# Softmax of the first two batches in five blocks, and signs, low parts and additions made by GpSimd

## The chip, the cores and the metric

The kernel runs on one core of a Trainium2 chip. The metric is the device time of one execution in microseconds (us). TensorE (PE) multiplies and has its weights loaded by a path of its own (PEld); VectorE (DVE), ScalarE (ACT) and GpSimd (POOL) do the elementwise work; SyncE (SP) issues nearly all transfers. Each engine runs its own instructions in program order and waits on semaphores for the others.

## The reference

All tensors are float32. For 8 batches of 8 heads, 576 positions and head size 64, keys and values are pooled into 32 slots per head; queries attend to the slots; the result goes through a feed-forward layer of width 2048.

```python
a = softmax(phi, axis=2)                          # phi (8, 8, 576, 32)
k_m = einsum('bhsm,bhsd->bhmd', a, k)             # v_m the same with v
attn = softmax(q @ k_m.T / sqrt(64))              # (8, 8, 576, 32)
x = (attn @ v_m).transpose(0, 2, 1, 3).reshape(4608, 512)
h = x @ w_in                                      # w_in (512, 2048)
g = where(h > 0, h, exp(min(h, 0)) - 1)
out = g @ w_out                                   # w_out (2048, 512)
```

`w_in` and `w_out` arrive as float64; the kernel reads them as pairs of 32-bit words.

## The kernel before, in words

**Products.** The value product and `w_in` are fused: for each batch `vw` multiplies the pooled values with `w_in`, and `hidden` multiplies the attention weights `A` with `vw`. `hidden` and `project` are made three times over split operands: a high part that ScalarE rounds, and a low part, the difference, that VectorE subtracts (`vw_high` and `vw_low`, `probs_high` and `probs_low`, `elu_high` and `elu_low`, `dec_high` and `dec_rest`). The passes run low weights first, then the low part of the moving side, then both high.

**Steps.** One iteration `it` is a batch, a half of its positions and a tile `j` of 128 hidden channels: `hidden.it` (6 matmuls of 288 columns, L672), `elu_exp.it` (ScalarE, L687 and L688), `elu_max.it` (VectorE, L696), `rest_copy.it` (GpSimd copies the last 32 positions away, L715), `elu_high.it` (ScalarE, L719), `elu_low.it` (VectorE, L725), `project.it` (6 matmuls of 512 columns, L733). 256 iterations follow each other.

**Weights.** Tile `k` (32 of them, `w_in` and `w_out`) comes by `load_raw.k` as float64 words. `dec_mag.k` (ScalarE, L376) scales the upper word; `dec_top.k` (VectorE) takes its sign bit (L384) and ors it to the shifted magnitude (L385); `dec_low.k` (ScalarE, L380) scales the lower word; `dec_add.k` (VectorE, L397) adds it as an integer; for `w_out`, `dec_high.k` (ScalarE, L404) rounds and `dec_rest.k` (VectorE, L409) subtracts. Tiles 0 to 7 are `w_in` 0, `w_out` 0, `w_in` 1 and so on to `w_out` 3.

**Attention of batches 0 and 1.** The pooled keys come from `slots` (L465), `slots_copy` (L482), `slots_transpose` (L499) and `kv_copy` (L506), first for the keys (`K`) and then for the values (`V`) in batch 0. `scores.b.u` (L514) multiplies queries of unit `u`; then on VectorE `turn` (32x32 transposes, L547), `softmax_max` (L554), `softmax_shift` (L562), on ScalarE `softmax_exp` (L566), on VectorE `softmax_sum` (L572, L573, L575), `softmax_divide` (L583), `turn_back` (L589), then `probs_high` (L606) and `probs_low` (L614). Units are ranges of positions: `units(b)` gives four of 160, 128, 160 and 128 for batches 0 and 1, three of 192 for the others. A unit's scores have two halves side by side, so a unit of 160 is worked on as 320 elements.

**Order.** The string `FIRST` writes out the order of all steps of the first 64 iterations by hand; the rest comes from rules. Steps of one engine run in the order in which they stand. `warm_up.n` is n matmuls of the identity on TensorE (L812), whose results nobody reads; each shows as two records. `ph`, `kvt`, `raw` and `qh` are transfers that SP issues in order.

**Tuples.** `shift_on_pool`, `low_on_pool` and the like name units whose step GpSimd does instead of VectorE; all of them are empty.

Of the kernel before, what the change touches and what calls it, by code (L numbers as in the profile page):

```python
# [47 lines left out]
tables load_phi.0 load_kv0.K0 load_kv0.K1 load_kv0.T phi_max.0.0 load_raw.0 phi_exp.0.0  # L48
phi_max.0.1 phi_exp.0.1 load_half_q.0.0 warm_up.11 e_transpose.0.0 slot_scale.0 e_transpose.0.1
e_copy.0.0 load_kv0.V0 slots.0.0.K.y e_copy.0.1 e_transpose.0.2 slots.0.1.K e_copy.0.2 load_kv0.V1  # L50
slots.0.2.K slots.0.3.K dec_mag.0 slots.0.4.K load_raw.1 slots_copy.0.K dec_top.0 warm_up.2
slots_transpose.0.K kv_copy.0.K dec_low.0 load_raw.2 warm_up.1 scores.0.0.yz scores.0.1 turn.0.0
turn.0.1 softmax_max.0.0 warm_up.2 slots.0.0.V.y load_phi.1 softmax_max.0.1 slots.0.1.V
softmax_shift.0.0 softmax_shift.0.1 softmax_exp.0.0 dec_add.0 softmax_exp.0.1 load_raw.3 warm_up.1
slots.0.2.V softmax_sum.0.0 slots.0.3.V softmax_sum.0.1 slots.0.4.V load_raw.5 softmax_divide.0.0
dec_mag.1 softmax_divide.0.1 turn_back.0.0 slots_copy.0.V turn_back.0.1 load_half_q.0.1
probs_high.0.0 warm_up.3 slots_transpose.0.V dec_top.1 probs_high.0.1 dec_mag.2 probs_low.0.0
kv_copy.0.V dec_low.1 load_kv.1.0 warm_up.3 vw.0.0.0.128.yz probs_low.0.1 dec_top.2
vw_high.0.0.0.128 load_kv.1.1 vw_low.0.0.0.128 dec_low.2 dec_add.1 warm_up.4 hidden.0 dec_mag.3
dec_add.2 dec_high.1 load_raw.6 dec_top.3 vw.0.0.128.256 elu_exp.0 dec_mag.5 dec_rest.1  # L60
load_kv.1.2 dec_low.3 elu_max.0 scores.0.2.yz phi_max.1 vw_high.0.0.128.256 rest_copy.0
scores.0.3.hh elu_high.0 load_kv.1.3 vw_low.0.0.128.256 phi_exp.1.0 turn.0.2 load_kv.1.4
phi_exp.1.1 turn.0.3 load_raw.4 softmax_max.0.2 hidden.1 softmax_max.0.3 softmax_shift.0.2
e_transpose.1.0 softmax_shift.0.3 elu_exp.1 load_raw.7 slot_scale.1 dec_add.3 softmax_exp.0.2
# [906 lines left out]
```

## Time and profile before

| | us |
|---|---|
| median of 3 runs (lowest, highest) | 722.78 (721.74, 724.0) |
| the profiled execution | 722.7 |
| its span, first to last instruction | 720.9 |
| TensorE busy | 700.8 (97%) |
| VectorE busy | 465.0 (64%) |
| ScalarE busy | 460.7 (64%) |
| GpSimd busy | 45.6 (6%) |

1.8 us of the profiled execution lie outside its span. Busy shares are means over stages with different limits: the first 65 us are unlike the rest.

### The profile page before, as it was taken

To read this page: it belongs to the slowest core of one execution; us is meant where nothing else is said; L and a number is where in the kernel's file an instruction comes from. 1 tells how busy PE (TensorE), PEld (TensorE's weight loads), DVE (VectorE), ACT (ScalarE), POOL (GpSimd) and SP (SyncE) were. 2 spreads that over 40 slices of the span, in tenths; PEclk is the share of its full clock that TensorE was granted. 3 is DMA by queue.
4 is the path that set the end of the run, shared out by engine and by line. 5 is a ranking of instruction groups with operands and counts; after the bars stand their busy time and mean duration, and the time that the engine had idled before them with its cause. 6 is when DMAs were issued, how large, how long until landed. Compare 5 with 4: busy or idle time off the path is not lost.

```text
span 720.9 us, 13704 instructions
## 1 busy us (share of the span) xinstructions
PE 700.8 (97%) x5114; PEld 575.8 (80%) x5114; DVE 465.0 (64%) x1253; ACT 460.7 (64%) x1110; POOL 45.6 (6%) x88
## 2 busy tenths in 40 slices
PE   7698999999999999999999999999999999999997
PEld 6576888888767888888887888888878888788886
DVE  3999899887495548664773547854593545945442
ACT  3778998886546756675564755765564655656652
POOL 0001112112100100010000100001000010000000
PEclk8799999999999999999999999999999999999999
DMA  8960503432312710343003430046000360000001
GB/s 304 367 257 9 226 30 117 151 104 63 103 60 81 184 51 1 96 135 101 0 1 110 132 104 1 0 109 193 30 1 33 85 197 31 1 30 1 30 1 45
DMA packets 24978, 64.46 MB, mean 89 GB/s; under 512 B 3408, under 2 KB 7632, under 8 KB 24912
## 3 DMA queue, kind: packets, MB, share of 16 engines
q1 hardware_dynamic: 24816, 63.46, 27.6%
q8 instruction: 41, 0.67, 0.4%
q14 instruction: 25, 0.20, 0.1%
q10 hardware_dynamic: 96, 0.13, 0.1%
...
## 4 chain that ended last, share of the span: by engine, by line
PE 87%; DVE 8%; DMA 2%; ACT 1%; issue 1%; SPq 0%; POOL 0%; DVEq 0%; POOLq 0%; ACTq 0%
PE pso L733 53%; PE psh L672 27%; PE psb L514 3%; PE psb L465 2%; PE pso L514 2%; DMA kvt<-kvt 1%; DMA e<-phi 1%; DVE gf L696 1%; DVE top L385 1%; DVE sm L572 1%; DVE vw L634 0%; DVE top L397 0%; DMA nmd<-nm 0%; DVE gp L725 0%; DVE mx L554 0%
## 5 line engine op out<-in xcount | busy, mean ns | idle before, releaser
L733 PE MATMUL pso<-wout,gp 128*128 128x512 f32 x1728 | 448.4, 397 | 3.7 <-DVE gp L725 2.3
L733 PEld LDWEIGHTS pso<-wout,gp 128*128 128x128 f32 x1728 | 309.0, 188 | 69.6 <-DVE gp L725 4.2
L672 PEld LDWEIGHTS psh<-A,vw 128*128 128x128 f32 x1536 | 230.9, 189 | 36.8 <-issue 10.2
L672 PE MATMUL psh<-A,vw 128*128 128x288 f32 x1536 | 248.7, 297 | 3.6 <-DVE spare L547 1.9
L699 DVE SCALAR_TENSOR_TENSOR gf<-gf,psh 128x256 f32<-128x256 f32 x192 | 80.7, 420 | 145.3 <-ACT gf L688 145.0
L687 ACT ACTIVATE gf<-psh 128x288 f32<-128x288 f32 x256 | 104.8, 409 | 106.6 <-PE psh L672 104.8
L719 ACT CAST gp<-gf 128x256 fp32r<-128x256 f32 x256 | 103.5, 405 | 81.2 <-DVE gf L699 65.9
L725 DVE TENSOR_TENSOR gp<-gf,gp 128x256 fp32r<-128x256 f32 x256 | 109.1, 427 | 50.2 <-ACT gp L719 49.5
L688 ACT ACTIVATE gf<-gf 128x288 f32<-128x288 f32 x256 | 113.9, 445 | 8.1
L290 POOL TENSOR_TENSOR e<-e,nmb 128x512 f32<-128x512 f32 (+1 forms) x18 | 20.8, 1180 | 367.9 <-DMA nmb<-nmd 204.0
L696 DVE SCALAR_TENSOR_TENSOR gf<-gf,psh 128x288 f32<-128x288 f32 x64 | 28.9, 452 | 17.4 <-ACT gf L688 16.2
L715 POOL COPY rest<-gf 128x32 f32<-128x32 f32 x64 | 24.3, 379 | 167.3 <-DVE gf L696 167.3
L707 DVE SCALAR_TENSOR_TENSOR rest<-gf,psh 128x32 f32<-128x32 f32 x192 | 34.6, 180 | 0.0
L634 DVE TENSOR_TENSOR vw<-psb,vw 128x512 fp32r<-128x512 f32 (+2 forms) x52 | 28.4, 569 | 1.9 <-ACT vw L628 1.8
L777 ACT CAST gp<-rest 128x256 fp32r<-128x256 f32 x32 | 12.6, 405 | 24.2 <-PE pso L733 22.5
L628 ACT CAST vw<-psb 128x512 fp32r<-128x512 f32 (+2 forms) x52 | 23.7, 486 | 0.7 <-PE psb L514 0.7
L514 PE MATMUL psb<-win,kvm 64*32 64x512 f32 (+2 forms) x416 | 23.8, 511 | 0.3 <-DVE win L397 0.3
L782 DVE TENSOR_TENSOR gp<-rest,gp 128x256 fp32r<-128x256 f32 x32 | 13.1, 419 | 16.2 <-ACT gp L777 16.1
L385 DVE SCALAR_TENSOR_TENSOR top<-mag,top 128x512 uint32<-128x512 uint32 x32 | 22.2, 692 | 1.9 <-ACT mag L376 0.3
L380 ACT ACTIVATE mag<-raw 128x512 uint32<-128x512 uint32 x30 | 20.0, 670 | 3.3 <-DVE top L385 3.3
L376 ACT ACTIVATE mag<-raw 128x512 f32<-128x512 f32 x30 | 19.5, 665 | 0.4 <-DVE win L397 0.4
L634 DVE TENSOR_TENSOR vw<-pso,vw 128x512 fp32r<-128x512 f32 (+1 forms) x26 | 16.0, 620 | 0.0
...
## 6 DMA issues: line engine op xcount, KB each, us to landing
...
```

The source lines that it names most:

```text
L385: nc.vector.scalar_tensor_tensor(t, mags[k].bitcast(U32), 3, t, ALU.logical_shift_left, ALU.bitwise_or)
L514: nc.tensor.matmul(outs[a][32 * j : 32 * j + 32, :], lhs[r, 32 * j : 32 * j + 32], rhs[r, j], start=True, stop=True, tile_position=(64 * a ...
L634: nc.vector.tensor_tensor(t[:, LO, a, n0:n1], s["ps"]["vw", c, n0][a], t[:, HI, a, n0:n1], ALU.subtract)
L672: nc.tensor.matmul(ps, t[:, x, g, c0 : c0 + P], s["A"][hf][:, y, g, :], start=(n == 0), stop=(n == 5),)
L687: nc.scalar.activation(gf, ps, AF.Relu, scale=-1.0)
L688: nc.scalar.activation(gf, gf, AF.Exp, scale=-1.0)
L696: nc.vector.scalar_tensor_tensor(gf, gf, -1.0, ps, ALU.add, ALU.max)
L699: nc.vector.scalar_tensor_tensor(gf[:, :n], gf[:, :n], -1.0, ps[:, :n], ALU.add, ALU.max)
L707: nc.vector.scalar_tensor_tensor(rest_of(b, j)[:, o : o + REST], gf[:, n:], -1.0, ps[:, n:], ALU.add, ALU.max)
L719: nc.scalar.copy(gp[:, HI], gs[it][:, : NT * P])
L725: eng.tensor_tensor(gp[:, LO], gf[:, : NT * P], gp[:, HI], ALU.subtract)
L733: nc.tensor.matmul(ps, gp[:, y], wout[j][:, x, :], start=(first and n == 0), stop=(last and n == 2),)
```

## The change

- `units` gives batch 0 three units (160, 128 and 288 positions) and batch 1 two of 288: five blocks in place of eight.
- The sign of a weight tile is a step of its own, `dec_sign.k`. For 19 tiles GpSimd makes it as the upper word, read as float32, times zero, which leaves a zero with the word's sign. The other 13 keep the mask on VectorE. It is written to where the tile will stand, so that `dec_top` and `dec_add` work in place.
- `dec_rest` is done by GpSimd for 8 of 16 tiles of `w_out`, `dec_add` for 6 of 32 tiles. Three of five `probs_low` and one `softmax_shift` of batches 0 and 1 go to GpSimd too.
- `FIRST` is written anew.

```diff
+    shift_on_pool = ((1, 0),)
+    low_on_pool = ((0, 0), (0, 2), (1, 0))
+    rest_on_pool = (1, 3, 7, 14, 15, 23, 29, 30)
+    sign_on_pool = (1, 3, 7, 9, 10, 11, 15, 16, 17, 19, 20, 21, 22, 23, 24, 26, 27, 29, 30)
+    add_on_pool = (0, 20, 23, 24, 26, 30)
...
     def units(b):
-        if b < NB:
-            return (0, 160), (160, 288), (288, 448), (448, 576)
+        if b == 0:
+            return (0, 160), (160, 288), (288, 576)
+        if b == 1:
+            return (0, 288), (288, 576)
         return (0, 192), (192, 384), (384, 576)
...
+    def dec_sign(k):
+        t = made(k)
+        word = raws[k][:, :, 1].rearrange("p (r n) -> p r n", r=NPAIR)
+        if k in sign_on_pool:
+            nc.gpsimd.tensor_scalar(t, word.bitcast(F32), 0.0, None, ALU.mult)
+        else:
+            nc.vector.tensor_scalar(t.bitcast(U32), word, 0x80000000, None, ALU.bitwise_and)
+
     def dec_top(k):
-        t = t2k([P, CW], "top").bitcast(U32)
-        nc.vector.tensor_scalar(t, raws[k][:, :, 1], 0x80000000, None, ALU.bitwise_and)
+        t = made(k).bitcast(U32)
+        mag = mags[k].bitcast(U32).rearrange("p (r n) -> p r n", r=NPAIR)
         nc.vector.scalar_tensor_tensor(
-            t, mags[k].bitcast(U32), 3, t, ALU.logical_shift_left, ALU.bitwise_or
+            t, mag, 3, t, ALU.logical_shift_left, ALU.bitwise_or
         )
...
+        eng = nc.gpsimd if k in add_on_pool else nc.vector
+        eng.tensor_tensor(t, t, lows.pop(k).rearrange("p (r n) -> p r n", r=NPAIR), ALU.add)
...
+        eng = nc.gpsimd if k in rest_on_pool else nc.vector
+        t = tops.pop(k).rearrange("p r n -> p (r n)")
+        eng.tensor_tensor(w[:, LO, :], t, w[:, HI, :], ALU.subtract)
```

Three places show what `FIRST` and the tuples move. Lines of the changed kernel stand some 15 higher than before.

TensorE, from the last key slots of batch 0 (`kvt,spare`) over the transpose of the pooled keys (`ident,spare`) to its first scores (`qh,kvm`), before:

```order
L465 MATMUL pso_133<-kvt,spare 32x64 x32
L812 MATMUL pso_84<-ident 128x128 x2
L499 MATMUL psb<-ident,spare 128x128
L812 MATMUL pso_84<-ident 128x128
L514 MATMUL pso_199<-qh,kvm 32x160 x4
```

and in the changed kernel:

```order
L480 MATMUL pso_134<-kvt,spare 32x64 x24
L827 MATMUL pso_84<-ident 128x128 x5
L514 MATMUL psb<-ident,spare 128x128
L529 MATMUL pso_204<-qh,kvm 32x160 x4
```

Five identity matmuls stand ahead of the transpose where two stood, and none behind it. SP's queue changes there too: the transfer of the last slots' rows (`kvt`) went ahead of the first weight tile (`win_78`) before:

```order
L311 DMA kvt<-kv 128x1024 x2
L309 DMA kvt<-kvt 64x1024
L368 DMA win_78<-w_in 128x1024
L340 DMA qh<-q 128x1152
```

and goes behind it in the changed kernel:

```order
L311 DMA kvt<-kv 128x1024 x2
L368 DMA win_78<-w_in 128x1024
L309 DMA kvt<-kvt 64x1024
L340 DMA qh<-q 128x1152
```

VectorE, from the sums of batch 0's last softmax to `elu_low.0` (`gp<-gf,gp`), before (two units of 160 and 128 positions):

```order
L572 TENSOR_REDUCE sm<-spare 128x8
L573 TENSOR_SCALAR sm<-sm 128x8
L575 RECIPROCAL rs<-sm 128x8
L583 TENSOR_TENSOR spare<-spare,rs 128x320
L409 TENSOR_TENSOR wout_485<-top,wout_485 128x512
L583 TENSOR_TENSOR spare<-spare,rs 128x256
L589 STREAM_TRANSPOSE spare<-spare 128x320
L589 STREAM_TRANSPOSE spare<-spare 128x256
L384 TENSOR_SCALAR top<-raw 128x512
L385 SCALAR_TENSOR_TENSOR top<-mag,top 128x512
L614 TENSOR_TENSOR A<-spare,A 128x2x160
L384 TENSOR_SCALAR top<-raw 128x512
```

and in the changed kernel (one unit of 288):

```order
L598 TENSOR_TENSOR spare<-spare,rs 128x576
L604 STREAM_TRANSPOSE spare<-spare 128x576
L397 TENSOR_SCALAR top<-raw 128x512
L402 SCALAR_TENSOR_TENSOR top<-mag,top 128x512
L397 TENSOR_SCALAR win_77<-raw 128x4x128
L402 SCALAR_TENSOR_TENSOR win_77<-mag,win_77 128x4x128
L740 TENSOR_TENSOR gp<-gf,gp 128x256
```

`dec_rest.3` (`wout_485`) and `probs_low` are gone from between them. They stand on GpSimd, whose queue began with `rest_copy` before and now begins like this (`A<-spare,A` is `probs_low`, `wout` is `dec_rest`, TENSOR_SCALAR is `dec_sign`, `win_80<-win_80,mx` is `softmax_shift.1.0`):

```order
L409 TENSOR_TENSOR win_77<-win_77,mag 128x4x128
L395 TENSOR_SCALAR top<-win_78 128x512
L629 TENSOR_TENSOR A<-spare,A 128x2x160
L395 TENSOR_SCALAR top<-raw 128x512
L423 TENSOR_TENSOR wout_362<-top,wout_362 128x512
L629 TENSOR_TENSOR A<-spare,A 128x576
L423 TENSOR_TENSOR wout_457<-top,wout_457 128x512
L730 COPY rest<-gf 128x32 x2
L395 TENSOR_SCALAR top<-raw 128x512
L730 COPY rest<-gf 128x32 x2
L577 TENSOR_TENSOR win_80<-win_80,mx 128x576
L395 TENSOR_SCALAR win_78<-raw 128x4x128
```

Some copies moved far back: `rest_copy.18` now stands behind `elu_high.41`, `rest_copy.32` behind `elu_max.45`.

## Rows read from the trace of the kernel before

**Rows 1.** Busy time of each engine in three stretches (us from the span's start), with its number of instructions, then the granted TensorE clock, the DMA share and GB/s.

```profile
15.00:65.00 50.00, 40.02 (x509) 30.39 (x494) 48.57 (x138) 36.12 (x90) 2.75 (x9) 0.86 0.69 250
70.00:180.00 110.00, 109.97 (x698) 90.08 (x698) 94.80 (x201) 92.61 (x217) 20.05 (x46) 1.00 0.36 114
230.00:710.00 480.00, 480.00 (x3335) 402.19 (x3334) 279.70 (x812) 293.35 (x714) 17.42 (x15) 1.00 0.21 62
```

**Rows 2.** Timeline of PE from 39 to 65 us: start, duration, what, count, and in brackets the idle time before it and what ended it. The row at 39.55 is `hidden.3`, those at 46.92 and 49.49 are `hidden.5` and `hidden.6`, those at 59.36 and 63.78 are `project.5` and `project.6` from their second matmul on.

```profile
39.55 1.15 PE L672 MATMUL psh<-A,vw 128*128 128x288 f32 x6
...
46.92 1.06 PE L672 MATMUL psh<-A,vw 128*128 128x288 f32 x6 [0.37 <-DVE gf L696]
...
49.49 1.13 PE L672 MATMUL psh<-A,vw 128*128 128x288 f32 x6 [0.86 <-DVE vw L634]
...
59.36 1.43 PE L733 MATMUL pso<-wout,gp 128*128 128x512 f32 x5 [1.27 <-DVE gp L725]
...
63.78 1.43 PE L733 MATMUL pso<-wout,gp 128*128 128x512 f32 x5 [1.06 <-DVE gp L725]
```

**Rows 3.** Timeline of VectorE at three points: the first `turn`, `elu_low.0` and `elu_low.6`.

```profile
15.00 0.35 DVE L547 STREAM_TRANSPOSE spare<-pso 128x160 f32<-128x160 f32 x1 [1.39 <-PE pso L514]
...
39.76 0.42 DVE L725 TENSOR_TENSOR gp<-gf,gp 128x256 fp32r<-128x256 f32 x1
...
63.31 0.41 DVE L725 TENSOR_TENSOR gp<-gf,gp 128x256 fp32r<-128x256 f32 x1
```

**Rows 4.** Timeline of PE from 11 to 24 us: the last key slots, identity matmuls, the transpose of the pooled keys, the first scores, and identity matmuls behind the first `vw` product.

```profile
11.27 0.43 PE L465 MATMUL pso<-kvt,spare 64*32 64x64 f32 x16 [0.59 <-DMA kvt<-kvt]
11.63 1.15 PE L812 MATMUL pso<-ident 128*128 128x128 f32 x4
13.34 0.47 PE L499 MATMUL psb<-ident,spare 128*128 128x128 f32 x1 [0.56 <-ACT spare L482]
...
14.17 0.79 PE L514 MATMUL pso<-qh,kvm 64*32 64x160 f32 x16
...
22.66 1.16 PE L812 MATMUL pso<-ident 128*128 128x128 f32 x8
```

**Rows 5.** Timeline of ScalarE: the first `dec_mag`, which waited for the first weight tile.

```profile
12.21 0.67 ACT L376 ACTIVATE mag<-win 128x512 f32<-128x512 f32 x1 [3.13 <-DMA win<-w_in]
```

**Rows 6.** Busy time by stretch as in rows 1, for two stretches of half clock.

```profile
11.70:18.50 6.80, 6.24 (x89) 4.63 (x93) 4.59 (x13) 3.29 (x8) 0.00 (x0) 0.50 1.02 408
28.90:39.00 10.10, 7.56 (x84) 6.44 (x87) 9.46 (x31) 8.10 (x19) 0.21 (x1) 0.50 1.03 334
```

**Rows 7.** Groups of VectorE instructions by line and shape, from 15 to 65 us: count, busy time, mean ns of one, idle time before.

```profile
L397 DVE CUSTOM_DVE_ANT_0 win<-top,mag 128x1024 uint16<-128x1024 uint16 x4 | 2.7, 684 | 0.0
L409 DVE TENSOR_TENSOR wout<-top,wout 128x512 fp32r<-128x512 f32 x4 | 2.7, 682 | 0.0
L384 DVE TENSOR_SCALAR top<-raw 128x512 uint32<-128x512 uint32 x6 | 2.5, 415 | 0.0
L614 DVE TENSOR_TENSOR A<-spare,A 128x320 fp32r<-128x320 f32 x2 | 1.0, 484 | 0.0
L614 DVE TENSOR_TENSOR A<-spare,A 128x256 fp32r<-128x256 f32 x2 | 0.8, 420 | 0.0
L573 DVE TENSOR_SCALAR sm<-sm 128x8 f32<-128x8 f32 x4 | 0.7, 172 | 0.1
L575 DVE RECIPROCAL rs<-sm 128x8 f32<-128x8 f32 x4 | 0.8, 204 | 0.1
```

**Rows 8.** Groups of VectorE by line and shape over the whole span: `softmax_max` of 384 and of 256 elements.

```profile
L554 DVE TENSOR_REDUCE mx<-sc 128x12 f32<-128x384 f32 x18 | 9.8, 545 | 0.0
L554 DVE TENSOR_REDUCE mx<-spare 128x8 f32<-128x256 f32 x2 | 0.8, 408 | 0.0
```

**Rows 9.** Groups of GpSimd by line and shape over the whole span.

```profile
L715 POOL COPY rest<-gf 128x32 f32<-128x32 f32 x64 | 24.3, 379 | 167.3 <-DVE gf L696 167.3
L290 POOL TENSOR_TENSOR e<-e,nmb 128x512 f32<-128x512 f32 x12 | 16.1, 1365 | 367.9 <-DMA nmb<-nmd 204.0 <-ACT gf L687 86.9 <-DVE gp L725 74.6
L290 POOL TENSOR_TENSOR e<-e,nmb 64x256 f32<-64x256 f32 x6 | 4.9, 811 | 0.0
```

**Rows 10.** Timelines of GpSimd and of VectorE around 320 us: three additions of GpSimd (two of 512 elements, one of 256, the last two in one row), and the `elu_low` of VectorE before and beside them.

```profile
319.13 1.31 POOL L290 TENSOR_TENSOR e<-e,nmb 128x512 f32<-128x512 f32 x1 [74.39 <-DMA nmb<-nmd]
320.39 2.21 POOL L290 TENSOR_TENSOR e<-e,nmb 128x512 f32<-128x512 f32 x2
...
318.83 0.43 DVE L725 TENSOR_TENSOR gp<-gf,gp 128x256 fp32r<-128x256 f32 x1
...
320.75 1.24 DVE L725 TENSOR_TENSOR gp<-gf,gp 128x256 fp32r<-128x256 f32 x1 [0.38 <-ACT gp L719]
```

**Rows 11.** Timelines of GpSimd and VectorE at 83 and at 88 us: a `rest_copy` beside `dec_add` and `elu_low`, and one beside `vw_low`.

```profile
82.95 0.61 POOL L715 COPY rest<-gf 128x32 f32<-128x32 f32 x1 [1.84 <-DVE gf L696]
...
82.81 0.69 DVE L397 CUSTOM_DVE_ANT_0 win<-top,mag 128x1024 uint16<-128x1024 uint16 x1
83.41 0.43 DVE L725 TENSOR_TENSOR gp<-gf,gp 128x256 fp32r<-128x256 f32 x1
...
88.28 0.21 POOL L715 COPY rest<-gf 128x32 f32<-128x32 f32 x1 [2.71 <-DVE gf L696]
...
88.14 0.75 DVE L634 TENSOR_TENSOR vw<-psb,vw 128x256 fp32r<-128x256 f32 x2
```

More of the change, by code (lines that the diff above doesn't have):

```diff
@@ L47 @@
 FIRST = """
[L48 to L64, printed above, removed]
-e_transpose.1.1 softmax_exp.0.3 elu_max.1 dec_mag.6 softmax_sum.0.2 load_half_q.1.0 rest_copy.1
@@ new lines @@
+dec_sign.1 dec_top.1 turn_back.0.0 turn_back.0.1 dec_mag.2 probs_high.0.0 probs_high.0.1 load_kv.1.0
+load_raw.5 load_half_q.0.1 warm_up.4 vw.0.0.0.128.yz vw_high.0.0.0.128 dec_sign.2 dec_top.2
+probs_low.0.0 dec_low.1 load_raw.6 vw_low.0.0.0.128 probs_low.0.1 dec_add.1 hidden.0 dec_mag.3
+dec_low.2 elu_exp.0 dec_high.1 dec_sign.3 dec_top.3 dec_add.2 vw.0.0.128.256 dec_mag.5 dec_rest.1
+load_kv.1.3 load_kv.1.1 load_kv.1.2 load_half_q.1.1 load_raw.4 elu_max.0 phi_max.1
+vw_high.0.0.128.256 dec_low.3 scores.0.2.yz vw_low.0.0.128.256 phi_exp.1.0 phi_exp.1.1 turn.0.2
@@ new lines @@
+softmax_max.0.2 hidden.1 e_transpose.1.0 elu_exp.1 load_raw.7 slot_scale.1 softmax_shift.0.2
+e_transpose.1.2.y e_transpose.1.1 dec_mag.6 softmax_exp.0.2 dec_add.3 elu_max.1 load_half_q.1.0
+e_copy.1.1 softmax_sum.0.2 dec_high.3 elu_high.1 e_copy.1.0 elu_high.0 softmax_divide.0.2
+turn_back.0.2 probs_high.0.2 probs_low.0.2 dec_rest.3 e_copy.1.2 slots.1.0 slots.1.1 slots.1.2
+slots.1.3 slots.1.4 dec_sign.5 rest_copy.0 dec_top.5 dec_mag.4 dec_low.5 dec_sign.4 dec_top.4
+dec_mag.7 dec_low.4 elu_low.0 hidden.3 slots_copy.1 dec_add.5 project.0 dec_add.4 elu_low.1
@@ new lines @@
+elu_exp.3 elu_max.3 elu_high.3 dec_high.5 vw.0.0.256.384.yz project.1 dec_sign.6 dec_top.6
+rest_copy.3 vw_high.0.0.256.384 vw_low.0.0.256.384 slots_transpose.1 dec_low.6 kv_copy.1 hidden.4
+elu_low.3 dec_add.6 dec_sign.7 dec_top.7 hidden.2 elu_exp.4 scores.1.0 elu_max.4 dec_low.7
+rest_copy.4 rest_copy.1 dec_rest.5 hidden.5 elu_high.4 elu_exp.2 turn.1.0 vw.0.0.384.512 elu_exp.5
+elu_max.2 softmax_max.1.0 vw_high.0.0.384.512 elu_high.2 vw_low.0.0.384.512 scores.1.1.yz elu_low.2
+hidden.6 elu_max.5 turn.1.1 softmax_shift.1.0 elu_exp.6 elu_low.4 softmax_exp.1.0 dec_add.7
@@ new lines @@
+load_raw.30 load_raw.13 elu_low.6 elu_max.8 probs_high.1.1 elu_exp.10 project.6 probs_low.1.1
+rest_copy.7 hidden.9 collect.6.0 elu_high.8 elu_low.7 project.7 collect.6.1 elu_max.10
+vw_low.1.0.256.512 hidden.12 elu_high.10 elu_low.10 elu_low.8 elu_exp.9 elu_max.9 dec_sign.9
+dec_sign.8 dec_top.9 load_raw.14 load_raw.15 load_raw.16 hidden.11 dec_mag.10 dec_top.8 rest_copy.9
+rest_copy.8 rest_copy.10 rest_copy.5 elu_high.9 collect.7.0 project.8 collect.7.1 elu_low.9
+project.9 elu_exp.11 dec_low.8 dec_sign.12 dec_top.12 elu_max.11 dec_add.8 elu_exp.12 elu_max.12
@@ L172 @@
+probs_low.2.1 rest_low.0.6 probs_low.2.0 rest_project.0.6 softmax_divide.2.2 rest_low.0.7
+turn_back.2.2 hidden.64 vw_low.2.1 probs_high.2.2 rest_project.0.7
 """
```

237 lines of the change are left out of this document (111 added, 126 removed).

## The prediction

> **What bounds the kernel now.** I read busy time by stretch first. From 230 to 710 us TensorE is busy all the time, from 70 to 180 for 109.97 of 110 [rows 1]; nothing that VectorE is spared there can show. The stretch from 15 to 65 us is different: VectorE is busy for 48.57 of 50 us, TensorE for 40.02 with its matmuls' modelled ends, at a mean clock of 0.86 [rows 1]. So the time is decided by when TensorE comes out of this head and is fed without a gap.
>
> Then I read TensorE's timeline there. From `hidden.3` at 39.55 it is short of work four times, 0.37, 0.86, 1.27 and 1.06 us, together 3.56, and each time a result of VectorE ends the wait; the last is `elu_low.6`, 63.31 to 63.72, for which `project.6` goes on at 63.78 [rows 2, 3]. From 70 to 180 us waits are 0.03 in all [rows 1]. The question is therefore what the change does to the end of `elu_low.6`. VectorE's stream for it starts with the first `turn` at 15.00 [rows 3].
>
> **What leaves VectorE.** Instructions in its stream overlap by 0.08 (0.69 from 82.81, the next at 83.41) [rows 11], so each counts by its mean less 0.08. Ahead of `elu_low.0`: one `dec_add` 0.60, two signs 0.34 each, two `dec_rest` 0.60 each, `probs_low` of unit (0,0) 0.40, and of units 2 and 3, now one, 0.40 and 0.34 [rows 7]: 3.6. Merging two units: 128 elements more cost 545 - 408 = 137 ns, so an instruction of 256 has 134 ns that do not depend on size [rows 8], 0.054 after the overlap; seven kinds of VectorE instruction run once less (two `turn`, max, shift, sum, divide, back), 0.38, and the small pair of the sum falls, 0.172 + 0.204 with its gaps [rows 7], 0.4. That is 0.8 a pair. Out ahead of `elu_low.0`: 4.4. Between it and `elu_low.6`: a sign 0.34, a `dec_rest` 0.60, a `probs_low` and a shift of a merged unit (taken alike) 0.74 each, two merges 1.6: 4.0.
>
> **What GpSimd takes for it.** Its additions of 512 take 1.31 us where nothing holds them [rows 10]; means are 1365 and 811 ns for 512 and 256 [rows 9]. With 1.31 and 0.74 (2.21 less 1.31, less 0.16 of waiting) one element costs 2.2 ns and the rest is 0.17. So `dec_rest` and `dec_add` are 1.31, a merged `probs_low` or shift of 576 is 1.45, and unit (0,0) of 320 is 0.88. A product with a constant stands in no row. Below it lies the copy of 32 elements, 0.21 alone [rows 11], above it 1.31. One input in place of two is half as much to read, so I take 1.1 ns an element and 0.17: 0.73. That is the nearer guess; both ends stay for the range.
>
> **What GpSimd's work costs VectorE.** The row that decides is at 320.75: `elu_low`, 0.43 at 318.83, takes 1.24, because it was issued 0.36 after GpSimd's second addition began, and ends after it [rows 10]. The other way round, a copy that takes 0.21 beside `vw_low`, which reads PSUM and one SBUF tile, takes 0.61 beside `dec_add`, and ends 0.06 after it [rows 11]. So GpSimd and a VectorE instruction with two SBUF inputs exclude each other, and whole instructions are waited for. In the order of the changed kernel I asked for each long GpSimd instruction which VectorE instruction comes next:
> - `dec_add.0` and `dec_sign.1` come before or beside `turn` and max, which have one input: nothing. `dec_rest.1` beside `phi_max.1` and the transposes: nothing. `dec_rest.7` beside `vw_low` and max: nothing.
> - `dec_sign.3` ahead of `probs_low.0.1` and `dec_add.1`: 0.85.
> - `probs_low.0.2` and `dec_rest.3`, back to back, while VectorE has only signs, tops and `elu_low.0` to do: 1.45 and 1.31, and `elu_low.0` stands behind them.
> - `dec_sign.7` ahead of `dec_top.6`: 0.73. `softmax_shift.1.0` ahead of `elu_low.2`, less 0.4 of `vw_low` beside it: 1.05. `probs_low.1.0` ahead of the tail of a sum, less 0.75 of reduction: 0.7.
>
> That is 3.6 ahead of `elu_low.0` and 2.5 behind it. By the rows alone only the two-input additions are seen to hold VectorE; then the signs' 0.85 and 0.73 fall away, and the sum below is 1.6 lower, 721.1. The Trainium skill, "SBUF — State Buffer", section "SBUF: two separate sides", says that the pair of ports is locked for a whole instruction and that any GpSimd instruction which reads SBUF contends with VectorE instructions of two SBUF inputs or of a two-port mode. By that rule the signs count too. I count them, since a one-input copy of GpSimd was made to wait [rows 11].
>
> **What comes late.** The last key slots waited for `kvt` until 11.27, the first weight tile was there at 12.21 [rows 4, 5]. With the two transfers exchanged I put the slots at 12.2. Behind them five identity matmuls, ten records, now stand ahead of the transpose. At the half clock of that stretch, 0.50 [rows 6], four records took 1.15 [rows 4]: ten take 2.9, and the transpose starts at 12.2 + 0.4 + 2.9 = 15.5, against 13.34 [rows 4]. About 0.2 of that was waiting anyway, so the first `turn` is 1.9 late. At full clock (8 records in 1.16 [rows 4]) it would be 0.8. A half more is waited for `vw` of batch 0, since `warm_up.4`, 1.16, now stands ahead of it: 0.9 with the wait for `dec_mag.2`.
>
> The exchange of `phi_max` costs nothing: it is hidden by the slots, which wait for their second transfer of keys, now the one that is needed first; without that cover it is one instruction, 0.75 us. The other moved loads cost nothing, since VectorE and not the queue is late from 40 us on; without that cover one place in the queue is 0.52 MB at 408 GB/s [rows 6], 1.3 us. New waits of TensorE for GpSimd are `hidden.3` for `probs_low.0.2`, with `project.0` behind it, and `project.1` for `dec_rest.3`; both come no later than `elu_low.0` and `elu_low.1`, which these projects need anyway. The late `rest_copy` leave two or three of five `gf` buffers to `elu_exp`; TensorE's work hides it, and where it does not, a wait is one GpSimd instruction, 1.31.
>
> **Sum.** `elu_low.0`: + 1.9 + 0.9 + 3.6 - 4.4 = 2.0 later. From there to `elu_low.6`: 2.5 - 4.0 = 1.5 earlier. Part of VectorE's own 1.4 of idle time [rows 1] takes up some of the waits: - 0.5. Together 0.0. The profiled execution of 722.7 stays 722.7, beside a median of 722.78.
>
> **The rivals.**
> *VectorE really is relieved.* GpSimd's instructions may fall beside one-input work oftener than I placed them. Without any holding `elu_low.6` would come 6 us earlier; but TensorE had only 3.56 us of waits to give back [rows 2], and about 0.5 from starting `hidden.3` sooner: 722.7 - 4.1 = 718.6. For it: TensorE's waits all end with VectorE. Against: the 1.24 us row.
> *GpSimd makes VectorE the bound from 70 to 180 us.* VectorE is busy for 94.80 of 110 there [rows 1]. Sixteen signs, five `dec_rest` and five `dec_add` leave, 13.5 by their means [rows 7]; 28.7 are then free. GpSimd adds 16 signs and 10 two-input instructions. At 0.73 they are 24.8, and fit even if each holds VectorE throughout; at 1.31 they are 34.1, 5.4 too much, and the time is 728. It decides from 0.98 us a sign, with full holding. Against: VectorE's `elu_max` and `vw_low` have one SBUF input.
> *The head is only half held.* Between my case and the first: 720.6.
>
> **How the numbers follow.** A measurement of this kernel tells about 0.3%, 2.2 us, from no change. My case 0.43, the relieved VectorE 0.27, the half-held head 0.13, VectorE as the bound 0.17. Faster takes the first rival, half of the third and 0.03 of mine: 0.36; slower the second and 0.06 of mine: 0.23; the same 0.41. The likeliest is 722.7; its own range is 720.8 to 724.6, from full clock in the head and signs that hold nothing on one side to signs of 1.31 on the other. Eight times in ten the time should lie between 718.0 and 726.5.
>
> **What would show it.** Right: the first `turn` near 17 us; `elu_low` or `dec_top` rows of over 1 us beside GpSimd's TENSOR_TENSOR; TensorE's last wait for `elu_low.6` ending near 63.7; no wait of TensorE from 70 to 180. Wrong: `elu_low.6` before 61, or signs of GpSimd above 1 us with TensorE waiting for `gp` after 70 us.

## The result, and the profile after

The changed kernel takes 726.38 us (median of 5 runs, 726.07 to 729.28), the kernel before 722.78: a ratio of 1.0053, 95% interval 1.0037 to 1.007, 3.6 us slower. Run once more beside other kernels it took 726.68, ratio 1.0041 (1.0029 to 1.0053). The forecast was 722.7 and no change, with 720.8 to 724.6 as its own range; the time lies above that, and just inside the wider range of 718.0 to 726.5.

The profiled execution of the changed kernel is its longest, 729.28 us with a span of 727.5 (before: 720.9). Busy time by stretch, as in [rows 1]; columns are the stretch, its length, busy us (and instructions) of TensorE, its weight loads, VectorE, ScalarE and GpSimd, then TensorE's granted clock, the DMA share and GB/s:

```profile
15.00:65.00 50.00, 43.08 (x479) 32.41 (x478) 42.60 (x92) 33.88 (x82) 21.23 (x20) 0.78 0.74 269
70.00:180.00 110.00, 108.06 (x678) 86.56 (x677) 88.94 (x174) 91.76 (x215) 51.46 (x71) 1.00 0.31 100
230.00:710.00 480.00, 480.00 (x3363) 400.86 (x3363) 281.85 (x814) 294.40 (x716) 17.39 (x15) 1.00 0.22 65
```

From 70 to 180 us TensorE now lacks 1.94 us of work (0.03 before), although VectorE is busy for only 88.94 of 110 us and GpSimd for 51.46. None of the engines that feed it is full there. From 15 to 65 us VectorE is busy for 42.60 of 50 us (48.57 before), so it no longer fills the head either, and TensorE's granted clock is 0.78 in the mean (0.86 before). TensorE's timeline between 64 and 190 us, the pieces that begin with a wait (start, us, line, tiles, then the idle time ahead and what ended it; `hidden` is now L687, `project` L748, `elu_max` L711):

```profile
65.80 1.43 PE L748 MATMUL pso<-wout,gp 128*128 128x512 f32 x5 [0.67 <-DVE gp L740]
98.78 1.07 PE L687 MATMUL psh<-A,vw 128*128 128x288 f32 x6 [0.31 <-DVE gf L711]
104.09 1.07 PE L687 MATMUL psh<-A,vw 128*128 128x288 f32 x6 [0.65 <-DVE gf L711]
141.03 1.07 PE L687 MATMUL psh<-A,vw 128*128 128x288 f32 x6 [0.65 <-DVE gf L711]
158.65 1.06 PE L687 MATMUL psh<-A,vw 128*128 128x288 f32 x6 [0.26 <-DVE gf L711]
188.17 1.99 PE L748 MATMUL pso<-wout,gp 128*128 128x512 f32 x6 [1.14 <-ACT gp L734]
```

Four of these waits are `hidden` waiting for VectorE's `elu_max`. What VectorE itself waited for from 70 to 180 us (what for whom: us in total, times, the longest):

```profile
DVE win L402 <- POOL win L395: 3.7, 5, 1.7
DVE top L402 <- POOL top L395: 3.5, 2, 1.9
```

L395 is `dec_sign` on GpSimd, L402 is `dec_top`, which now is one instruction. VectorE stands 7.2 us waiting for signs that GpSimd has not finished. GpSimd's groups (count, busy us, mean ns of one):

```profile
L395 POOL TENSOR_SCALAR top<-raw 128x512 f32<-128x512 f32 x9 | 14.4, 1606 | 0.0
L395 POOL TENSOR_SCALAR win<-raw 128x512 f32<-128x512 f32 x9 | 14.3, 1591 | 3.1 <-DVE win L409 3.1
L423 POOL TENSOR_TENSOR wout<-top,wout 128x512 fp32r<-128x512 f32 x8 | 10.9, 1367 | 6.2 <-ACT wout L416 6.2
...
L409 POOL TENSOR_TENSOR top<-top,mag 128x512 uint32<-128x512 uint32 x3 | 4.2, 1387 | 2.7 <-ACT mag L380 2.5
```

A sign takes 1.6 us, where the forecast had 0.73 and 1.31 as its upper bound; the two-input instructions cost what [rows 9, 10] said. One of the waits in full, GpSimd first, then VectorE; what it does to TensorE is the row at 104.09 above:

```profile
100.68 0.77 POOL L730 COPY rest<-gf 128x32 f32<-128x32 f32 x2 [0.72 <-DVE gf L711]
101.42 1.52 POOL L395 TENSOR_SCALAR win<-raw 128x512 f32<-128x512 f32 x1
```

```profile
100.54 0.69 DVE L409 CUSTOM_DVE_ANT_0 win<-win,mag 128x1024 uint16<-128x1024 uint16 x1
102.98 0.69 DVE L402 SCALAR_TENSOR_TENSOR win<-mag,win 128x512 uint32<-128x512 uint32 x1 [1.74 <-POOL win L395]
103.58 0.45 DVE L711 SCALAR_TENSOR_TENSOR gf<-gf,psh 128x288 f32<-128x288 f32 x1
```

In the order `dec_sign.17` stands directly ahead of `dec_top.17`, and on GpSimd behind two `rest_copy`, the first of which can only start when `elu_max.22` is done at 100.62. So the sign starts at 101.42, `dec_top.17` waits 1.74 for it, `elu_max.23` stands behind `dec_top.17`, and `hidden.25`, which waits for `elu_max.23`, goes on at 104.09.

### The profile page after: what moved, and what is told of

Same layout as the page of the kernel before. It is cut to its first block, busy times and chain, and to the rows that moved or that the text cites. A ratio compares the mean times of both kernels' runs of the same rounds, so it can differ in the third digit from the quotient of the medians.

```text
span 727.5 us, 13535 instructions
## 1 busy us (share of the span) xinstructions
PE 705.3 (97%) x5066; PEld 577.0 (79%) x5066; DVE 459.2 (63%) x1186; ACT 459.6 (63%) x1104; POOL 96.4 (13%) x125
## 4 chain that ended last, share of the span: by engine, by line
PE 80%; DVE 6%; ACT 5%; DMA 3%; issue 3%; POOL 2%; SPq 0%; DVEq 0%; ACTq 0%; POOLq 0%
PE pso L748 48%; PE psh L687 24%; PE psb L480 3%; PE psb L529 3%; PE pso L529 2%; DMA kvt<-kvt 1%; DVE gp L740 1%; DVE gf L711 1%; ACT gp L734 1%; DMA e<-phi 1%; PE pso L827 1%; ACT gf L703 1%; ACT gf L702 1%; POOL win L395 1%; POOL top L395 1%
## 5 line engine op out<-in xcount | busy, mean ns | idle before, releaser
L748 PE MATMUL pso<-wout,gp 128*128 128x512 f32 x1728 | 447.0, 397 | 3.3 <-ACT gp L734 1.1
L748 PEld LDWEIGHTS pso<-wout,gp 128*128 128x128 f32 x1728 | 309.6, 188 | 70.8 <-DVE gp L740 3.3
L687 PEld LDWEIGHTS psh<-A,vw 128*128 128x128 f32 x1536 | 229.8, 189 | 39.7 <-issue 11.9
L687 PE MATMUL psh<-A,vw 128*128 128x288 f32 x1536 | 248.9, 298 | 3.9 <-DVE gf L711 2.4
L740 DVE TENSOR_TENSOR gp<-gf,gp 128x256 fp32r<-128x256 f32 x256 | 118.3, 464 | 57.0 <-ACT gp L734 55.6
L711 DVE SCALAR_TENSOR_TENSOR gf<-gf,psh 128x288 f32<-128x288 f32 x64 | 28.5, 449 | 12.4 <-ACT gf L703 11.1
L730 POOL COPY rest<-gf 128x32 f32<-128x32 f32 x64 | 21.5, 353 | 77.0 <-DVE gf L711 76.8
L797 DVE TENSOR_TENSOR gp<-rest,gp 128x256 fp32r<-128x256 f32 x32 | 13.1, 419 | 16.2 <-ACT gp L792 16.1
L480 PE MATMUL psb<-kvt,e 128*32 128x128 f32 (+1 forms) x480 | 15.8, 275 | 0.0
```

The costliest lines, as they stand in the source:

```text
L480: nc.tensor.matmul(ps[32 * j : 32 * j + 32, a], s["e"][c // 2][:r, c % 2, x : x + M], kv_rows(b, c, i, 2 * j + a), start=(c == 0 and a == ...
L687: nc.tensor.matmul(ps, t[:, x, g, c0 : c0 + P], s["A"][hf][:, y, g, :], start=(n == 0), stop=(n == 5),)
L711: nc.vector.scalar_tensor_tensor(gf, gf, -1.0, ps, ALU.add, ALU.max)
L740: eng.tensor_tensor(gp[:, LO], gf[:, : NT * P], gp[:, HI], ALU.subtract)
L748: nc.tensor.matmul(ps, gp[:, y], wout[j][:, x, :], start=(first and n == 0), stop=(last and n == 2),)
```

## The experiments

Starts of `project.10`, `project.53` and `project.56` on TensorE's timeline, less those of the kernel before (72.43, 174.54, 181.20), tell where a kernel loses. All profiled executions in one table, worked out from the timelines, in the order of the growth between the first two:

```
kernel                          p.10    p.53   growth   p.56    ratio of times (95%)
e4_old_order_gp                +0.96   +9.56   8.60   +10.90   1.0144 (1.0124 to 1.0165)
e10_sign_of_mag                -1.55   +2.95   4.50    +4.16   1.0050 (1.0039 to 1.0062)
the changed kernel             +1.95   +5.75   3.80    +6.97   1.0053 (1.0037 to 1.0070)
e2_head_back                   +2.81   +6.60   3.79    +7.65   1.0091 (1.0075 to 1.0108)
e11_after_again                -0.65   +3.10   3.75    +4.22   1.0041 (1.0029 to 1.0053)
e15_raw2_first                 -0.79   +2.93   3.72    +4.40   1.0062 (1.0046 to 1.0077)
e12_signs_back                 +0.22   +2.57   2.35    +3.10   1.0029 (1.0016 to 1.0042)
e1_late_back                   +0.76   +2.23   1.47    +2.23   1.0015 (1.0004 to 1.0025)
e3_all_back                    +1.86   +3.27   1.41    +3.19   1.0040 (1.0025 to 1.0056)
e6_warmups_back                -1.34   +0.04   1.38    +0.17   1.0001 (0.9989 to 1.0013)
e7_loads_back                  -0.12   +1.25   1.37    +1.17   1.0006 (0.9997 to 1.0016)
e9_early_signs_old_head        +1.39   +2.19   0.80    +2.49   1.0009 (0.9998 to 1.0021)
e5_early_signs                 -0.89   -0.12   0.77    +0.68   1.0009 (1.0000 to 1.0018)
e8_before_new_warmups          +2.02   +2.06   0.04    +1.99   1.0012 (0.9999 to 1.0024)
e13_old_late_order             -0.35   -0.35   0.00    -0.05   0.9984 (0.9973 to 0.9994)
e14_old_late_order_raw2        -0.76   -0.82  -0.06    -0.90   0.9979 (0.9970 to 0.9988)
```

The growth is the same within 0.1 us wherever the late stretch is the same, whatever the head did. `project.10` differs by 2.6 us between two executions of the unaltered kernel, so of the head the ratios are read, not one profile; the granted clock from 15 to 65 us was 0.78 in the one and 0.88 in the other (e11). Of the 3.80 us that the changed kernel grows, 1.9 are waits of TensorE. Between the two steps it has as many matmuls as before, and the other 1.9 lie in the spacing of their starts (`hidden` 1.1, `project` 0.7), where the profile shows it busy.

**Which of GpSimd's work costs,** that of the head or that behind it, and what is left without any of it.

```diff
 e1_late_back
-    rest_on_pool = (1, 3, 7, 14, 15, 23, 29, 30)
-    sign_on_pool = (1, 3, 7, 9, 10, 11, 15, ... 29, 30)
-    add_on_pool = (0, 20, 23, 24, 26, 30)
+    rest_on_pool = (1, 3, 7)
+    sign_on_pool = (1, 3, 7)
+    add_on_pool = (0,)
```

> GpSimd keeps only what it does for tiles 1, 3 and 7, dec_add.0 and the three softmax instructions in the head; all signs, rests and additions of tiles 9 and up are VectorE's again. Theory of late waits: in the changed kernel VectorE waits 7.2 us for GpSimd's signs between 65 and 190 us, and TensorE starts there later and later (1.95 us behind the kernel before at project.10, 5.5 at project.50); without these signs the lag stays at about 2 from project.10 to project.50, and the time is 724.5 (723.7 to 725.5). Theory of the head: all of the 3.6 us are lost before 65 us, what GpSimd does later is hidden behind TensorE; the time stays 726.4.

Measured 723.86 against 723.32, 1.0015. In the profile TensorE has one wait between 65 and 190 us in place of the five behind 66 us above:

```profile
125.92 1.07 PE L687 MATMUL psh<-A,vw 128*128 128x288 f32 x6 [0.21 <-DVE gf L711]
```

This is the theory of late waits; that of the head falls. But a growth of 1.47 stays, which that theory did not have.

```diff
 e2_head_back
-    shift_on_pool = ((1, 0),)
-    low_on_pool = ((0, 0), (0, 2), (1, 0))
-    rest_on_pool = (1, 3, 7, 14, 15, 23, 29, 30)
-    sign_on_pool = (1, 3, 7, 9, 10, 11, 15, ... 29, 30)
-    add_on_pool = (0, 20, 23, 24, 26, 30)
+    shift_on_pool = ()
+    low_on_pool = ()
+    rest_on_pool = (14, 15, 23, 29, 30)
+    sign_on_pool = (9, 10, 11, 15, ... 29, 30)
+    add_on_pool = (20, 23, 24, 26, 30)
```

> The reverse: GpSimd keeps the signs, rests and additions of tiles 9 and up, all of its head work (signs 1, 3, 7, rests 1, 3, 7, dec_add.0, three low parts, one shift) is VectorE's again. If GpSimd's holding of VectorE is what makes the head late (rows of 1.65, 1.60 and 1.16 us where 0.42 to 0.74 would do, about 3.3 us ahead of elu_low.6), the head gets earlier and the time falls to about 723.5. If the late start does it and GpSimd's head work is a net relief (6.0 us of VectorE's work against 3.3 of holding), elu_low.6 comes about 2.5 later, and the time is 728.5 (727.5 to 730).

1.0091: GpSimd's head work is a net relief of about 3 us (2.7 to 3.6 by the two ratios of the changed kernel). The same five late waits stand in its trace, four of them within 0.05 us of those above, the last 0.97.

```diff
 e3_all_back
     shift_on_pool, low_on_pool, rest_on_pool, sign_on_pool, add_on_pool: all = ()
```

> No GpSimd work at all; the new order, its loads and the five blocks stay. By late waits and late start: the gain of the first run and the loss of the second, 726.5 (725 to 728), with no wait of TensorE from 75 to 180 us. By the head's holding: 723.5, or less. If the two sum to the before time, 722.8, order and blocks cost nothing and GpSimd is the whole of it.

1.0040: with no GpSimd work the new order still costs 2.9 us. `project.53` is 1.41 later behind `project.10` than before. So the order and the five blocks, without any GpSimd work, are a part of the loss of their own.

```diff
 e4_old_order_gp
     FIRST, units(b) and the spare layouts of the kernel before, dec_sign.k ahead of each dec_top.k;
     all tuples of the changed kernel
```

> The order, the loads and the eight blocks of the kernel before, with every GpSimd assignment of the change (each dec_sign stands just ahead of its dec_top). By late waits and late start: the first turn is at 15.0 again, the head gains up to 2.5 us, the waits for signs cost 2 to 4 after 65 us: 722.7 (721.5 to 725). By the head's holding: later than before already at project.7, and the time is 725 or more.

733.1, 1.0144: 8 us above the range of the first expectation. The second allowed any time from 725 and a head that is late at `project.7`, and it is, by 0.98; but the other 9.9 us are lost between `project.10` and `project.56`, where VectorE waits 14.9 us for signs, twice what it does in the changed kernel. Without an order made for them, the signs cost more still.

**When the sign starts, or that GpSimd works at all.**

```diff
 e5_early_signs: 13 or 14 steps earlier for tiles 10, 15, 16, 17, 19 to 24, 26, 27, 29, 30; here 17
+ dec_sign.17
  dec_rest.15 elu_exp.22 elu_low.21 elu_max.22 rest_copy.22 rest_copy.21 ... project.21 dec_add.16
- dec_sign.17
  dec_top.17
```

> The changed kernel with 14 of GpSimd's signs (tiles 10 and 15 to 30) put 14 places earlier in the order, ahead of the rest_copy and dec_rest that they stood behind; the same work on the same engines. If VectorE stands waiting because a sign of 1.6 us is started just when its dec_top is due, the 7.2 us of VectorE's waits for signs fall to under 1.5, TensorE's lag behind the kernel before grows by less than 2 from project.10 to project.53 (3.8 in the changed kernel), and the time is 724.3 (723.5 to 725.3). If GpSimd's work costs by occupying the SBUF access that VectorE shares, whenever it runs, nothing changes: 726.4.

724.1, 1.0009: 2.3 to 3.2 us less than the changed kernel (by its two ratios) for the same work on the same engines. That is more than taking these signs from GpSimd altogether gave back (e12 below), since VectorE then makes them itself. The rows of the same place as above, in this kernel (GpSimd, VectorE, TensorE):

```profile
93.18 1.72 POOL L395 TENSOR_SCALAR win<-raw 128x512 f32<-128x512 f32 x1
```

```profile
97.74 0.68 DVE L409 CUSTOM_DVE_ANT_0 win<-win,mag 128x1024 uint16<-128x1024 uint16 x1
98.45 0.73 DVE L402 SCALAR_TENSOR_TENSOR win<-mag,win 128x512 uint32<-128x512 uint32 x1
```

```profile
100.14 0.96 PE L687 MATMUL psh<-A,vw 128*128 128x288 f32 x6
```

The sign is done 3.5 us before `dec_top.17` wants it, and `hidden.25` starts without a wait. No wait for a sign is left among VectorE's waits from 65 to 185 us; of GpSimd it waits for one addition:

```profile
DVE win L409 <- POOL win L409: 0.4, 1, 0.4
```

**What makes a sign dear.**

```diff
 e10_sign_of_mag, for 12 late tiles
-            nc.gpsimd.tensor_scalar(t, word.bitcast(F32), 0.0, None, ALU.mult)
+            word = word.bitcast(F32)
+            if k in sign_of_mag:
+                word = mags[k].rearrange("p (r n) -> p r n", r=NPAIR)
+            nc.gpsimd.tensor_scalar(t, word, 0.0, None, ALU.mult)
```

> The changed kernel, but twelve of GpSimd's late signs (tiles 9, 10, 17, 19, 20, 22, 23, 24, 26, 27, 29, 30) are taken from the scaled copy in mag, which lies without gaps and has the same sign, and not from every second word of raw; the other signs stay on raw. If the stride of two words is what makes a product of 512 dearer (1.54 us) than an addition of 512 (1.30), the twelve fall to 0.7 to 1.3, VectorE's waits for signs fall by 0.3 to 0.8 each, and the time to 724.5 to 726. If the price is the operation's own: still 1.54, and 726.4.

`word` is every second word of a float64 tile; `mags[k]` is ScalarE's scaled copy of it, contiguous and of the same sign. The price is the operation's own, not that of the stride:

```profile
L399 POOL TENSOR_SCALAR win<-mag 128x512 f32<-128x512 f32 x7 | 10.6, 1511 | 6.0 <-DVE win L413 3.2 <-ACT mag L377 2.8
L399 POOL TENSOR_SCALAR top<-mag 128x512 f32<-128x512 f32 x5 | 7.8, 1551 | 2.9 <-ACT mag L377 2.9
```

1.0050, as the changed kernel. The growth is 0.7 larger: such a sign cannot start before ScalarE's copy is there, and VectorE's waits for signs are 8.6 us in place of 7.2.

**Once more unaltered** (e11), to see what of the head is chance:

> The changed kernel once more, unaltered, beside the others on one chip. If the lag at the end of the head is only a matter of the execution (1.95 us at project.10 in the first profile, -0.89 in e5, whose head is the same), it lies between -1 and 2 here, while the growth from project.10 to project.56 is again 4 to 5 us, since it comes from the waits for signs. Time 726.4 (725.5 to 727.5).

`project.10` at -0.65 in place of +1.95, growth 3.75 and 3.80. In e11 the first `turn` is at 17.27, `elu_low.0` at 41.29 and `elu_low.6` at 62.71; in the first profile 18.43, 43.57 and 65.36; before, 15.00, 39.76 and 63.31 [rows 3].

**The late two-input instructions alone.**

```diff
 e12_signs_back
-    sign_on_pool = (1, 3, 7, 9, 10, 11, 15, ... 29, 30)
+    sign_on_pool = (1, 3, 7)
```

> The changed kernel with the signs of tiles 9 and up on VectorE again; GpSimd keeps its late additions and rests, the two-input instructions, and all of the head. If the late loss comes from waiting for signs: 724.2 (723.5 to 725), as in e1_late_back. If it comes from the late two-input instructions, which hold elu_low for up to 1.1 us each: 726, and VectorE, with the signs' 5.4 us on top, makes it no better.

1.0029, growth 2.35: between the expectations. The late signs, directly ahead of their `dec_top`, cost 1.4 us of growth, the five `dec_rest` and five `dec_add` 0.9 over e1. The second theory is right to that extent; how it goes is in these rows (GpSimd, VectorE, TensorE):

```profile
132.47 1.30 POOL L423 TENSOR_TENSOR wout<-top,wout 128x512 fp32r<-128x512 f32 x1 [0.79 <-ACT wout L416]
```

```profile
132.54 1.52 DVE L740 TENSOR_TENSOR gp<-gf,gp 128x256 fp32r<-128x256 f32 x1
```

```profile
138.55 1.07 PE L687 MATMUL psh<-A,vw 128*128 128x288 f32 x6 [0.60 <-DVE gf L711]
```

`elu_low.36`, issued 0.07 behind `dec_rest.23`, takes 1.52 in place of 0.42. The wait of 0.60 at 138.55 is absent in e1, where the rest is VectorE's. That the one leads to the other, six us later, is likely and not shown.

**The head without GpSimd's doing.** In the new order ten records of identity matmuls stand ahead of the first transpose, twelve ahead of `slots.0.4.V`, eight ahead of the first `vw`; before, four, none and six.

```diff
 e6_warmups_back (on e1_late_back)
- warm_up.1 warm_up.2 slots_transpose.0.K
+ slots_transpose.0.K ... warm_up.1
- warm_up.3 warm_up.3 slots.0.4.V ... slots_transpose.0.V ... warm_up.4 vw.0.0.0.128
+ slots.0.4.V ... warm_up.3 slots_transpose.0.V ... warm_up.3 vw.0.0.0.128 ... warm_up.4
```

> e1_late_back with the identity matmuls of the head where the kernel before has them: ten records out from ahead of the first transposes, twelve out from ahead of slots.0.4.V, eight from ahead of the first vw. If these matmuls lie on the path (1.5, 2.9 and 1.9 us at half clock in e1_late_back, while VectorE idles 4.7 us between 19 and 28 us), the first vw is 3 us earlier, at about 22.4, and the time is 721.5 (720.5 to 722.5), below the kernel before. If the wait for the values and the weights takes their place, 723.9 as e1_late_back.

1.0001, 1.0 us less than e1 and not the 2.4 expected, and the two intervals overlap. The first `vw` is at 22.32, where it was expected and 3.1 earlier than in e1; 2.1 of it is left at `project.10` in these two profiles. TensorE in e1 and then in e6, up to the first `vw`:

```profile
18.96 0.26 PE L480 MATMUL pso<-kvt,spare 128*32 128x64 f32 x1 [3.06 <-issue]
19.15 2.93 PE L827 MATMUL pso<-ident 128*128 128x128 f32 x12
...
23.57 1.92 PE L827 MATMUL pso<-ident 128*128 128x128 f32 x8
25.42 0.68 PE L529 MATMUL pso<-win,kvm 64*32 64x128 f32 x16
```

```profile
20.17 0.57 PE L480 MATMUL pso<-kvt,spare 128*32 128x64 f32 x17 [1.31 <-issue]
20.68 0.94 PE L827 MATMUL pso<-ident 128*128 128x128 f32 x6
...
21.56 0.83 PE L827 MATMUL pso<-ident 128*128 128x128 f32 x6
22.32 0.45 PE L529 MATMUL pso<-win,kvm 64*32 64x128 f32 x16
```

In both profiles TensorE stops ahead of these matmuls, for nothing that the profile names (last section). In e1 it stood still for 3.06 us, and the granted clock behind that, from 19.1 to 30 us, is 0.50; in e6 it is 1.00 from 19.1 to 25.4. So e1 has twenty records of identity matmuls behind the stop where e6 has twelve, and each of them takes longer, 0.24 us in place of 0.15. The profiles do not tell the one from the other.

```diff
 e8_before_new_warmups (on the kernel before): the same moves the other way
```

> The kernel before, with nothing changed but the places of the identity matmuls in the head, which stand as in the changed kernel. If they are on the path: the first vw about 3 us later than 22.27, of which VectorE's fuller stream lets at least 2 through to elu_low.6; 725.3 (724.3 to 726.5). If they only fill waits of TensorE: 723.

1.0012 (0.9999 to 1.0024), 0.9 us; in the profile the first `vw` is 2.66 later and `project.10` 2.02. This profile too has a stop, of 2.70, and a clock of 0.50 from 19.1 to 30 us; the kernel before has neither there. Both ways the move goes with about 1 us, which neither pair shows by itself: the interval of e8 reaches no change. Whether the matmuls cost it, or the half clock of these two executions, is open: from the end of the stop to the first `vw` both take 6.46 us, while e10, with the matmuls in the same places, a stop of 2.98 and a clock of 1.00 behind it, takes 3.90; and in e7, with the same places and no stop, the first `vw` is at 22.64, 0.37 later than before.

```diff
 e7_loads_back (on e1_late_back)
- phi_max.0.1 phi_max.0.0 load_kv0.K1 load_kv0.K0 load_raw.0 load_kv0.T
+ phi_max.0.0 phi_max.0.1 load_kv0.K0 load_kv0.K1 load_kv0.T load_raw.0
```

> e1_late_back with the first loads in the order of before (K0, K1, T, first weight tile) and phi_max exchanged back; the identity matmuls stay. By the prediction's term for the late transfer: 1.1 us less, 722.8. If the first turn is not what sets the end of the head (in e1_late_back it was at 14.28, ahead of the kernel before, and project.10 came 0.8 late all the same), no change: 723.9 (723.2 to 724.5).

1.0006 against 1.0015, intervals that overlap: unsettled, and not more than about 1 us.

```diff
 e15_raw2_first (on the changed kernel)
- load_raw.1 load_phi.1 load_kv.1.4 load_raw.2
+ load_raw.1 load_raw.2 load_phi.1 load_kv.1.4
```

> The changed kernel with this one load moved: load_raw.2 ahead of load_phi.1 and load_kv.1.4. By the prediction the moved loads cost nothing: 726.6, as the changed kernel. If the wait of dec_sign.2 for the third weight tile costs: hidden.0 about 1 us earlier than 25.14 to 27.44, and 725.3 to 726.

1.0062: no gain. `hidden.0` came at 23.80, 1.3 earlier than in e11, and `project.10` at the same place. The moved loads cost nothing, as forecast.

**Putting the better halves together.**

```diff
 e9_early_signs_old_head: e5 with the identity matmuls of e6 and the loads of e7
```

> The changed kernel with the early signs of e5 and, in the head, the loads and the identity matmuls where the kernel before has them. If both effects add (1.0053 to 1.0009 by the signs, about 1.0 us by the identity matmuls, up to 0.6 by the loads): 722.3 (721.3 to 723.3), 0.998 to 1.000 of the kernel before, with GpSimd's whole share of the work in it. If the head's gains are given back at e_shift.2, where the early-sign kernel waited 0.7 us: 723.5.

1.0009, later than both expectations: the effects did not add. Its profile is 1.39 late at `project.10`; that this is chance of the first loads, as in the changed kernel's two profiles, is possible and not shown.

```diff
 e13_old_late_order (on e6_warmups_back): behind project.10 the remaining steps in the order of before
```

> e6_warmups_back up to project.10, and from there the remaining steps in the order of the kernel before (every decoding step of tiles 9 and up that is still to do on VectorE). Without any GpSimd work there, e1, e6 and e7 still lost 1.4 us between project.10 and project.56. If the new order of these steps does that, the lag stays what it is at project.10 (-1.3 in e6) and the time is 721.6 (720.8 to 722.5), below the kernel before. If the loss comes of the head (buffers or loads that its order leaves late), it stays, and the time is 722.6 to 723.

721.87 against 723.03, 0.9984 (0.9973 to 0.9994). The growth is 0.00, and TensorE's pieces that begin with a wait between 62 and 190 us are two:

```profile
63.44 1.43 PE L749 MATMUL pso<-wout,gp 128*128 128x512 f32 x5 [0.33 <-DVE gp L741]
181.15 2.03 PE L749 MATMUL pso<-wout,gp 128*128 128x512 f32 x6 [0.22 <-ACT gp L735]
```

So the order of the steps behind `project.10` costs 1.4 us of growth without any GpSimd work. Only 0.25 of it is a wait of TensorE; the rest is spacing: from `project.10` to `project.53` the same 252 `hidden` matmuls take 1.1 us longer in e6 than here, and 14 times in e6, 6 times here, two in a row start over 0.19 us apart. Which of the moved steps does that was not tried.

```diff
 e14_old_late_order_raw2: e13 with the load of e15
```

> e13 with load_raw.2 ahead of load_phi.1 and load_kv.1.4 on SP, as in the kernel before. In all runs of the new order the third weight tile lands at 21.9 to 24.7 (19.17 before), and dec_sign.2 and dec_top.2 wait for it in VectorE's order ahead of the first vw_low, which hidden.0 waits for. If that wait sets the start of hidden.0: hidden.0 0.7 to 1.5 earlier than in e13 and 0.5 to 1 us less time. If the next wait takes its place, the same time as e13.

721.17, 0.9979 (0.9970 to 0.9988): with e13 the versions that beat both kernels, and not told apart from it. They keep the five blocks, the new order of the head but for the identity matmuls, and GpSimd's work in it; what the change does behind `project.10` they drop.

**The account**, from ratios times 723: the new head with GpSimd's work and the old places of the identity matmuls -1.2 (e13); the new order behind `project.10` +1.2 (e6 over e13); the new places of the identity matmuls +1.0 (e1 over e6); late rests and additions +1.0 (e12 over e1); late signs +0.9 to 1.7 (the changed kernel's two ratios over e12). Together +2.9 to 3.7, measured 3.0 and 3.8. The terms telescope, so the sum is no test, and each difference of two ratios is uncertain by about 1.2 us, as much as the terms themselves. What holds them up is the growth column, which repeats within 0.1 us, and for the signs e5 with the rows at 101 us; the term of the identity matmuls has no such support.

## Why the prediction was wrong, point by point

- **The price of a sign: wrong.** "One input in place of two is half as much to read, so I take 1.1 ns an element and 0.17: 0.73." In the mean of a group it is 1.5 to 1.7 us, above the upper bound of 1.31 from the two-input row. Here the instruction of one input is the dearer one. The Trainium skill, "GPSIMD Engine Reference", section "4.1 Engine selection", says that GpSimd's one-input work runs at roughly line rate while two-input work is about twice as slow as VectorE's; the product at 1.52 against an addition at 1.30 does not agree.
- **Whether GpSimd fits in from 70 to 180 us: the step that failed.** The rival there was worked out by throughput: so many us of GpSimd against VectorE's free 28.7, lost only above 0.98 us a sign, "with full holding". The place was right, the time it gave (728) near, the mechanism not. VectorE has 21 us idle in that stretch and still makes TensorE wait, because a result of 1.5 us is asked for at once: the order has the sign directly ahead of its `dec_top`, which became a wait of VectorE for GpSimd that it did not have before. The forecast asked of each GpSimd instruction whom it holds, and for the head alone also who waits for its result; its sum ends at `elu_low.6` and puts nothing behind it. Measured there are 1.94 us without work for TensorE from 70 to 180 us and a growth of 3.8 from `project.10` to `project.53`; with the signs early (e5) they are none and 0.8. "No wait of TensorE from 70 to 180" was wrong, and what the forecast had named as proof of the opposite came: signs above 1 us and TensorE waiting, though mostly `hidden` for `elu_max`, not `project` for `gp`.
- **The order behind 70 us: not priced.** Beside the late `rest_copy` the forecast asked of no step there what its new place costs; e13 shows 1.2 to 1.4 us in it.
- **What GpSimd's work holds up: too much.** Forecast 3.6 ahead of `elu_low.0` and 2.5 behind it; the rows that are longer than their kind give 0.45 (`dec_add.1`), 1.23 (`dec_sign.4`), 0.91 (`dec_top.4`) and 0.73 (`elu_low.2`), together 3.3. The place was right, in VectorE's rows and GpSimd's:

```profile
40.30 1.65 DVE L397 TENSOR_SCALAR win<-raw 128x512 uint32<-128x512 uint32 x1
42.05 1.60 DVE L402 SCALAR_TENSOR_TENSOR win<-mag,win 128x512 uint32<-128x512 uint32 x1
```

```profile
40.13 1.53 POOL L629 TENSOR_TENSOR A<-spare,A 128x576 fp32r<-128x576 f32 x1 [8.29 <-ACT A L621]
41.62 1.48 POOL L423 TENSOR_TENSOR wout<-top,wout 128x512 fp32r<-128x512 f32 x1
```

 With 6.0 us of work leaving VectorE (4.4 and 4.0 less the merges) that is a gain of 2.7; measured are 2.7 to 3.6 (e2 over the changed kernel) and 1.8 (e3 over e1). The signs, counted with 0.85 (more than the 0.73 that a sign was put at) and 0.73, held 0.45 and nothing. The mask at 40.30 has one input and took 1.65 all the same, usually 0.42: "two SBUF inputs" was too narrow for what is held. The Trainium skill's rule of the locked pair of ports ("SBUF — State Buffer", "SBUF: two separate sides") fits the two-input rows, and not the signs (last section).
- **The late start: right in kind, in size a matter of the execution.** Forecast: slots at 12.2, transpose 15.5, first `turn` 1.9 late. The profile:

```profile
13.96 0.65 PE L480 MATMUL pso<-kvt,spare 64*32 64x64 f32 x16 [2.85 <-DMA kvt<-kvt]
14.54 2.50 PE L827 MATMUL pso<-ident 128*128 128x128 f32 x10
16.84 0.42 PE L514 MATMUL psb<-ident,spare 128*128 128x128 f32 x1
```

 and the first `turn` 3.43 late at 18.43, because the slots' `kvt` came 1.8 later than put. The ten matmuls took 2.50, forecast 2.9. (For full clock the forecast's own numbers give 0.5 and not 0.8: ten records in 1.45, the transpose at 14.05.) In other runs with the same first loads `kvt` landed between 11.34 and 13.65, and the first `turn` in e1 was at 14.28, yet `hidden.0` was 2.5 late: TensorE stopped for 3.06 us, and behind that stood the next twelve and eight identity matmuls, at half clock 2.93 and 1.92. Of these the forecast counted only the eight, at 1.16, and of the stop nothing.
- **The head as a whole: 0.0 forecast**, -0.6 at `elu_low.6` in e11, +2.05 in the first profile. The two executions lie around the forecast, and differ by more than half of what was to be explained; that its sum came out near is in part luck, since the held time was put 2.8 too high, and the start too early. The lower end of its own range does not follow from the terms named for it: 722.7 less 1.6 and 1.1 is 720.0, not 720.8.
